# Six Winograd pairs per block and written-out operation lists in an attention and GeGLU kernel

## Chip, cores and metric

The kernel runs on one core of one Trainium2 chip. The metric is the device time of one execution in microseconds (us); the median of three runs stands for a kernel. Matrix products run on TensorE (PE), whose results land in PSUM; VectorE (DVE), ScalarE (ACT) and GpSimd (POOL) do the rest. SyncE (SP) issues the DMAs.

## What is computed

Linear attention over 8 batches with 8 heads, 576 rows and 64 columns each, and a gated feed-forward block on its output:

```python
def _attn_ref(q, k, v):
    q_s = softmax of q over the last axis
    k_s = softmax of k over the sequence
    kv = np.einsum('bhsd,bhse->bhde', k_s, v)
    return np.einsum('bhsd,bhde->bhse', q_s, kv)

def _moe_ref(x, w_gate, w_val, w_out):      # x: 4608 x 512, d_ff = 1536
    g = x @ w_gate
    gelu = 0.5 * g * (1.0 + erf(g * inv_sqrt2))
    val = x @ w_val
    return (gelu * val @ w_out).astype(np.float32)
```

All is float32 outside; inside, matmul operands are f16.

## The kernel before

The work goes through nine blocks of 512 rows: one per batch, 0 to 7, with the main 512 rows of the batch, and block 8 with the 64 remaining rows of each batch. They run in the order 0 to 6, 8, 7. A block has a gate part (12 tiles of 128 hidden columns, each `gelu(x w_gate) * (x w_val)`, into `ht`) and an output part (`ht` times `w_out`).

From block 1 on the output part (`out_strassen`, L755) is a seven-product Winograd scheme of 2 x 2 quarters. From block 2 on part of the gate is one too: hidden tiles k and k+3 are a *pair* (`pair_step`, L653), k one of 0, 1, 2, 6, 7, 8. A pair has seven products (`product_gv`, L619; matmuls at L629), each of four matmuls of 256 columns, in three PSUM banks:

- product 1 goes to bank a, which ACT copies to bank b (L686); products 6, 7, 4 accumulate in a, product 2 in b, products 5 and 3 in c (L629);
- a scaled snapshot of c after product 5 (*s5*) and of a after product 6 (*s2*) is taken to SBUF, by ACT (L666) or DVE (L664);
- DVE adds c to s2 after product 3, and a to s5 after product 7 (L670); ACT takes a Gelu of one half (L674), and POOL or DVE multiplies the two (L676): the rows 256 to 511 of both tiles;
- after product 2, and after product 4, ACT takes a 256-wide Gelu (L656) and DVE multiplies (L657): the rows 0 to 255.

A product may only write a bank after the snapshot, copy or add of its last state has read it. Tiles outside of pairs are computed directly (`half`, L643; matmuls at L471): 8 matmuls of 512 columns, a Gelu (L648) and a product (L650) each.

The pairs need sums of weight quarters (`sum_w1`, L604, two inputs in SBUF, 16 bits), made once for a pair's k; those for tile 7 are made in blocks 2 and 3, those for tile 8 in blocks 4 and 6, on DVE. They need four sums of x in each block (`sum_x`, L613, all on POOL), and the output part four sums of `ht` for each of three column groups (`sum_h`, L576, DVE or POOL).

Between these lies the attention of the next batches: exp of q and k (L210, ACT), row sums and reciprocals (`norm_pair`, L233, DVE), the scaling (`norm_mul`, L246, POOL), a cast of v (`cast_v`, L215, POOL), a DMA transpose of q (`unit_td`, L387, on SP), the k-v product (`unit_kv4`, L340) and x (`unit_x4`, L426), copied out of PSUM by ACT and DVE.

The order is set by hand. Each engine runs its instructions in program order; the program is emitted by walking a list of steps per block and "riding" other work on them (`at`, L949, and `ride`, L1034). Banks come from a ring of eight: `big(..., hold=True)` takes the next one and `let_go` puts it back at the end. The lists:

```python
FOUR = ("a 7g l 7v n 0.1 6.1 0.2 6.2 0.3 6.3 m p 10g 0.4 6.4 1.1 t 10v 1.2 8g 1.3 s0 8v u0 1.4 2.1"
        " 11g 2.2 11v 2.3 s1")
FIVE = ("a 8g l 8v n m 0.1 6.1 0.2 6.2 0.3 6.3 0.4 1.1 p 6.4 7.1 t 1.2 7.2 1.3 s0 7.3 2.1 1.4 u0 11g 2.2"
        " y 7.4 11v 2.3 s1")
...
steps = {b: (SIX if b >= B - 1 else FIVE if b > 3 else FOUR).split() for b in range(2, B + 1)}
```

`0.1` is the first step of pair 0, `7g` and `7v` the direct tile 7. So blocks 2 and 3 have pairs 0, 1, 2, 6 and four direct tiles; blocks 4 to 6 also have pair 7 and two direct tiles; blocks 8 and 7 have six pairs.

Of the kernel before, what the change touches and what calls it, by code (L numbers as in the profile page):

```python
# [18 lines left out]
def kernel(  # L19
# [12 lines left out]
    B, H, S, D = q.shape  # L32
    C = H * D
# [34 lines left out]
    def small(shape, dt, name):  # L68
        if not att_ring:
            return big(shape, dt, name)  # L70
        tag = att_ring.pop(0)
        att_ring.append(tag)
        full.discard(tag)
        return ps_big.tile(shape, dt, name=name, tag=tag)
# [18 lines left out]
    def let_go(t):  # L93
        ring.append(held.pop(id(t))[1])

# [176 lines left out]
    def norm_rem0():  # L272
        e = eq0r[0:64].rearrange("p (h d) -> p h d", d=D)
        rq = att.tile([64, H], f32, name="rq0", tag="rq0", bufs=1)
        nc.vector.reduce_sum(rq, e, axis=mybir.AxisListType.X)
        rrq = att.tile([64, H], f32, name="rrq0", tag="rrq0", bufs=1)
        nc.vector.reciprocal(out=rrq, in_=rq)
        nc.gpsimd.tensor_tensor(
            out=e, in0=e, in1=rrq.unsqueeze(-1).to_broadcast((64, H, D)), op=ALU.mult)
# [60 lines left out]
    def unit_kv4(b, spare=False):  # L340

        ps = bank([P, HP, VW], "pskv", spare)
        for hp in range(HP):
            for n in range(NC):
                for s in range(2):
                    c0 = hp * P + s * D
                    nc.tensor.matmul(  # L347
                        ps[s * D:(s + 1) * D, hp, :], ek_b[0][:, n, c0:c0 + D],
                        v16_b[0][:, n, 2 * hp + s, 0:VW], start=(n == 0), stop=(n == NC - 1))
        rck = att.tile([P, HP], f32, name="rck4", tag="rck4")  # L350
# [4 lines left out]
        st[(b, "kv4")] = kv  # L355

# [69 lines left out]
    def unit_x4(b, engs=("act", "dve"), rem=None):  # L426
# [19 lines left out]
        for s, eng in enumerate(engs):  # L446
            copy_on(eng, xtr[:, 2 * s:2 * s + 2, b * REM:(b + 1) * REM], psr[s][:, 0:2])
            if rem is not None:
                r = slice(64 * s, 64 * s + 64)
                copy_on("act" if b == B - 1 else eng, xtr[r, :, rem * REM:(rem + 1) * REM], psr[s][r, 2:])  # L450
        for i in range(2):
            ps = [big([P, MAIN], f32, "psx") for _ in range(2)]
            for hp in (2 * i, 2 * i + 1):
                go(ps, hp, xq(b, hp))
            for s, eng in enumerate(engs):
                copy_on(eng, xt[:, i + 2 * s, :], ps[s])
# [8 lines left out]
    def preload(func):  # L465
        nc.scalar.activation(out=tiny[:, 0:1], in_=tiny[:, 0:1], func=func)
# [7 lines left out]
    def gate(psg, psv, fi):  # L474
        gl = ffn.tile([P, 512], f32, name="gl", tag="gl")
# [137 lines left out]
    def sum_x(xt, xs=xs):  # L613
        b11, b12, b21, b22 = (xt[:, c:c + 2, r:r + 256] for c in (0, 2) for r in (0, 256))
        t = [xs[:, i] for i in range(4)]
        for o, a, b in ((t[0], b12, b11), (t[1], b22, t[0]), (t[2], b22, b12), (t[3], b21, t[1])):
            nc.gpsimd.tensor_tensor(out=o, in0=a, in1=b, op=ALU.subtract)

    def product_gv(i, ps, xt, k, first):  # L619
        lo, hi = slice(k * P, (k + 1) * P), slice((k + NO // 2) * P, (k + NO // 2 + 1) * P)  # L620
        xs = xs_b[xt is st.get((B - 1, "xt"))]
        for t, w, nm in ((0, wv_sb, "v"), (1, wg_sb, "g")):
# [11 lines left out]
    FOUR = ("a 7g l 7v n 0.1 6.1 0.2 6.2 0.3 6.3 m p 10g 0.4 6.4 1.1 t 10v 1.2 8g 1.3 s0 8v u0 1.4 2.1"  # L634
            " 11g 2.2 11v 2.3 s1")
    FIVE = ("a 8g l 8v n m 0.1 6.1 0.2 6.2 0.3 6.3 0.4 1.1 p 6.4 7.1 t 1.2 7.2 1.3 s0 7.3 2.1 1.4 u0 11g 2.2"
            " y 7.4 11v 2.3 s1")
    SIX = ("0.1 6.1 0.2 6.2 0.3 6.3 0.4 1.1 6.4 7.1 s0 1.2 7.2 1.3 u0 7.3 1.4 2.1 7.4 8.1 2.2"
           " 8.2 2.3 s1 8.3 2.4")
    steps = {b: (SIX if b >= B - 1 else FIVE if b > 3 else FOUR).split() for b in range(2, B + 1)}  # L640
    live = {}

    def half(b, xt, c, nm):  # L643
        t = big([P, 512], f32, "ps" + nm)
        mm_gv(t, wg_sb if nm == "g" else wv_sb, xt, c, range(HP))
        if nm == "g":
            live[c] = ffn.tile([P, 512], f32, name="gl", tag="gl")
# [5 lines left out]
    def pair_step(b, xt, k, i):  # L653
        def final(ps, fi):
            gl = ffn.tile([P, 256], f32, name="glq", tag="gl")
            nc.scalar.activation(out=gl, in_=ps[:, 1], func=ACTF.Gelu)  # L656
            nc.vector.scalar_tensor_tensor(out=ht[:, fi, 0:256], in0=ps[:, 0], scalar=_H_SCALE,  # L657
                                           in1=gl, op0=ALU.mult, op1=ALU.mult)
            let_go(ps)

        def snap(ps, dve=False):
            sn = ffn.tile([P, 2, 256], f32, name="snq", tag="snq")
            if dve:
                nc.vector.tensor_scalar(out=sn, in0=ps, scalar1=_H_SCALE, scalar2=None, op0=ALU.mult)  # L664
            else:
                nc.scalar.activation(out=sn, in_=ps, func=ACTF.Copy, scale=_H_SCALE)  # L666
            return sn

        def add(o, ps, sn):
            nc.vector.scalar_tensor_tensor(out=o, in0=ps, scalar=_H_SCALE, in1=sn,  # L670
                                           op0=ALU.mult, op1=ALU.add)

        def upper(cc):
            nc.scalar.activation(out=cc[:, :, 1], in_=cc[:, :, 1], func=ACTF.Gelu,  # L674
                                 scale=1.0 / _H_SCALE)
            (nc.vector if k == NFI - NO // 2 - 1 else nc.gpsimd).tensor_tensor(  # L676
                out=ht[:, k:k + NO // 2 + 1:NO // 2, 256:512], in0=cc[:, :, 0], in1=cc[:, :, 1],
                op=ALU.mult)

        if i == 1:  # L680
            live["odd"] = odd = not live.get("odd", True)
            cc = cc_b[b > 2] if odd else ffn.tile([P, 2, 2, 256], f32, name="cc", tag="cc", bufs=1)
            pa = big([P, 2, 256], f32, "pga", True)
            product_gv(1, pa, xt, k, True)
            pb = big([P, 2, 256], f32, "pgb", True, True)
            nc.scalar.copy(out=pb, in_=pa)  # L686
            pc = big([P, 2, 256], f32, "pgc", True)
            product_gv(5, pc, xt, k, True)
            live[k] = [cc, pa, pb, pc, snap(pc, b >= B - 1 or b > 3 and k % NO == 1)]
            return  # L690
        cc, pa, pb, pc, s5 = live[k]
        if i == 2:
            product_gv(6, pa, xt, k, False)
            s2 = snap(pa)
            product_gv(3, pc, xt, k, False)
            add(cc[:, 0], pc, s2)
            let_go(pc)
        elif i == 3:
            product_gv(7, pa, xt, k, False)
            add(cc[:, 1], pa, s5)  # L700
            product_gv(2, pb, xt, k, False)
            final(pb, k)
            if k == NFI - NO // 2 - 1 or 3 < b < B - 1 and k < 2 or 3 < b < B - 1 and k == NO:
                live["late"] = lambda: upper(cc)
            elif 3 < b < B - 1 and k == NO + 1:
                live["y"] = lambda: upper(cc)
            else:
                upper(cc)
        else:
            product_gv(4, pa, xt, k, False)  # L710
            if steps[b] and steps[b][0].endswith(".1"):
                live["late"] = lambda: final(pa, k + NO // 2)
            else:
                final(pa, k + NO // 2)

    def go_on(b, xt, upto=None):
        while steps[b] and upto != 0:
            x = steps[b].pop(0)
            late = live.pop("late", None) if "." in x else None
            if "." in x:  # L720
                k, i = x.split(".")
                pair_step(b, xt, int(k), int(i))
                upto = upto - 1 if upto else None
            elif x[-1] in "gv" and x[:-1].isdigit():
                half(b, xt, int(x[:-1]), x[-1])
            elif x == "y":
                live.pop("y")()
            else:
                ride(b, PR, x)
            if late:  # L730
                late()

# [19 lines left out]
    def last_js(b):  # L752
        return (NO - 2 if b < 2 else NO // 2 - 1, NO)

    def out_strassen(b, last):  # L755
        yo = [yop.tile([P, 2, C], f32, name="yo", tag="yo") for _ in range(2)]
        c = (slice(0, 256), slice(256, 512))
        ps, tiles_ = {}, {}

        def get(nm):  # L760
            if last:
                tiles_[nm] = [big([P, 256], f32, "ps" + nm, True) for _ in range(2)]
                ps[nm] = [x for x in tiles_[nm]]
            else:
                tiles_[nm] = [big([P, 2, 256], f32, "ps" + nm, True)]
                ps[nm] = [tiles_[nm][0][:, t] for t in range(2)]

        def parts(nm):
            return [(0, ps[nm][0]), (1, ps[nm][1])] if last else [(slice(0, 2), tiles_[nm][0])]

        def snap(nm, act=False):
            sn = ffn.tile([P, 2, 256], f32, name="sn", tag="gl")
            for n, (t, src) in enumerate(parts(nm)):
                if n or act:
                    nc.scalar.activation(out=sn[:, t], in_=src, func=ACTF.Copy, scale=1.0 / _H_SCALE)
                else:
                    nc.vector.tensor_scalar(out=sn[:, t], in0=src, scalar1=1.0 / _H_SCALE,  # L777
                                            scalar2=None, op0=ALU.mult)
# [321 lines left out]
```

The softmax here doesn't subtract the row's maximum and nothing guards it: scores larger than these inputs give would overflow.

## Time and profile before

| what | value |
|---|---|
| median of 3 runs | 292.18 us (292.15 to 292.21) |
| the profiled execution | 292.19 us |
| its span, first to last instruction | 290.3 us |
| POOL casting v, 128x640 (L186) | 26 times, mean 786 ns |
| ACT exp of one batch's k (L210), 128x2560 | mean 2324 ns |
| ACT table loads (L466, L210, L476) | 16, 1283 ns each |

The page gives busy time, share of the span and instruction count of each engine, then busy tenths in 40 slices. A row of the groups names line, engine, operation, out<-in with shapes and count, then total busy us, mean ns of one, and the idle time before it with what ended it. In the chain a piece is given by its start, its length and how many instructions it merges. In the stretches by block each number is the busy time of an engine with its instruction count in brackets.

### The profile page before, as it was taken

The numbers are of one execution on the slowest core, as the hardware profiler recorded it, in microseconds if no ns is written. First come the engines' busy times: TensorE is split into PE (matmuls) and PEld (weight loads), VectorE is DVE, ScalarE is ACT, GpSimd is POOL, SyncE is SP. The second block draws the span as 40 slices with busy tenths as digits, with TensorE's granted clock in tenths as the row PEclk, the third lists the DMA queues.
The fourth block names the chain that finished last, engine by engine and source line by source line (L and its number), as shares of the span: only waits on it lengthen the run. The fifth ranks groups of instructions, "written<-read, shape, count | busy, mean of one in ns | idle before, by whom it ended". The sixth has DMA issues, their size and how long they took to land.

```text
span 290.3 us, 6495 instructions
## 1 busy us (share of the span) xinstructions
PE 281.3 (97%) x2497; PEld 207.4 (71%) x2497; DVE 229.4 (79%) x430; ACT 197.8 (68%) x332; POOL 195.1 (67%) x180
## 2 busy tenths in 40 slices
PE   3999999999999999999999999999999999999994
PEld 1544445445877787768787878887888888888883
DVE  2854988877997779677988888887889689938982
ACT  3773367785787589757987698769773577537650
POOL 1567746987478569865996689669975476283640
PEclk9999999999999999999999999999999999999999
DMA  6999999999049903990299119911140110033003
GB/s 213 374 381 387 401 392 390 371 344 239 7 155 372 201 2 135 335 256 2 89 312 303 41 76 311 304 41 72 75 93 9 72 77 0 3 73 73 2 0 145
DMA packets 54622, 51.72 MB, mean 178 GB/s; under 512 B 18496, under 2 KB 50496, under 8 KB 54592
## 3 DMA queue, kind: packets, MB, share of 16 engines
q1 hardware_dynamic: 52864, 49.49, 54.3%
q10 hardware_dynamic: 1728, 1.84, 2.0%
q8 instruction: 19, 0.31, 0.4%
q14 instruction: 11, 0.09, 0.1%
HBM read 37.75 MB, written 9.44 MB: 163 GB/s over the span
## 4 chain that ended last, share of the span: by engine, by line
PE 95%; DVE 2%; ACTq 1%; ACT 1%; issue 0%
PE pga L629 21%; PE psa L745 14%; PE psg L471 11%; PE psv L471 11%; PE pgc L629 11%; PE psc L745 7%; PE pgb L629 5%; PE psb L745 4%; PE psy L539 4%; PE pswarm L463 2%; PE pskv L347 1%; PE psx L434 1%; ACTq L166 1%; DVE yo L783 1%; PE pst L372 1%; PE psx L413 1%
## 5 line engine op out<-in xcount | busy, mean ns | idle before, releaser
L629 PEld LDWEIGHTS <-wgv_sb 128*128 128x128 f16 x560 | 54.2, 98 | 10.7
L471 PEld LDWEIGHTS <-wgv_sb 128*128 128x128 f16 x304 | 29.5, 98 | 30.4 <-issue 0.8
L248 POOL TENSOR_TENSOR eq<-eq,rrq 128x640 f16<-128x640 f16 (+1 forms) x27 | 34.7, 1302 | 11.7 <-DVE rrq L240 8.2
L745 PEld LDWEIGHTS <-ht 128*128 128x128 f16 x384 | 36.6, 98 | 7.4 <-issue 2.5
L471 PE MATMUL psg<-xt,wgv_sb 128*128 128x512 f16 x152 | 41.1, 379 | 0.0
L471 PE MATMUL psv<-xt,wgv_sb 128*128 128x512 f16 x152 | 41.0, 379 | 0.0
L676 POOL TENSOR_TENSOR ht<-eq 128x512 f16<-128x512 f32 x17 | 21.6, 1272 | 19.7 <-ACT eq L674 19.6
L629 PE MATMUL pga<-xs,wgv_sb 128*128 128x256 f16 x232 | 34.5, 273 | 0.0
L656 ACT ACTIVATE glq<-pgb 128x256 f32<-128x256 f32 x35 | 13.3, 379 | 21.1 <-PE pgb L629 14.4
L586 POOL TENSOR_TENSOR s<-ht,sh 128x512 f16<-128x512 f16 x14 | 16.2, 1155 | 16.3 <-DVE sh L586 16.3
L476 ACT ACTIVATE gl<-psg 128x512 f32<-128x512 f32 x24 | 13.8, 597 | 16.8 <-PE psg L471 16.8
L676 POOL TENSOR_TENSOR ht<-cc 128x512 f16<-128x512 f32 x16 | 20.4, 1275 | 7.1 <-ACT cc L674 7.1
L186 POOL CAST v<-vt 128x640 f16<-128x640 f32 x26 | 19.4, 786 | 7.8 <-PE pskv L347 6.2
L686 ACT COPY pgb<-pga 128x512 f32<-128x512 f32 x35 | 20.4, 583 | 6.0 <-PE pga L629 5.6
L657 DVE SCALAR_TENSOR_TENSOR ht<-pga,glq 128x256 f16<-128x256 f32 x35 | 14.8, 422 | 12.0 <-ACT glq L656 11.8
L586 POOL TENSOR_TENSOR ht<-ht 128x512 f16<-128x512 f16 x16 | 18.9, 1188 | 8.0 <-DVE sh L586 8.0
L745 PE MATMUL psa<-tw,ht 128*128 128x256 f16 x192 | 23.4, 272 | 0.2
L477 DVE SCALAR_TENSOR_TENSOR ht<-psv,gl 128x512 f16<-128x512 f32 x24 | 16.0, 685 | 9.4 <-PE psv L471 7.7
L666 ACT ACTIVATE snq<-pga 128x512 f32<-128x512 f32 x35 | 20.9, 599 | 3.5 <-PE pga L629 3.2
L210 ACT ACTIVATE ek<-kt 128x1280 f16<-128x1280 f32 (+1 forms) x11 | 19.1, 1748 | 5.7 <-DMA kt<-in_k_dram 4.0
L238 DVE TENSOR_REDUCE rq<-eq 128x20 f32<-128x1280 f16 (+1 forms) x12 | 17.2, 1432 | 4.6 <-ACT eq L210 4.6
L745 PEld LDWEIGHTS <-sh 128*128 128x128 f16 x192 | 18.7, 98 | 2.5 <-DVE sn L777 0.3
(174 smaller groups left out, 683.0 us busy)
## 6 DMA issues: line engine op xcount, KB each, us to landing
out_dram<-yo SPq DMA_DIRECT2D x15, 512.0 KB, 3.4
kt<-in_k_dram SPq DMA_DIRECT2D x7, 640.0 KB, 8.5
vt<-in_v_dram SPq DMA_DIRECT2D x7, 640.0 KB, 5.6
qt<-in_q_dram SPq DMA_DIRECT2D x7, 640.0 KB, 7.7
qt<-in_q_dram SPq DMA_DIRECT2D x8, 512.0 KB, 7.9
wost<-in_moe_w_out_dram SPq DMA_DIRECT2D x6, 512.0 KB, 7.9
kt<-in_k_dram SPq DMA_DIRECT2D x6, 512.0 KB, 9.7
vt<-in_v_dram SPq DMA_DIRECT2D x6, 512.0 KB, 6.1
```

What stands on the lines that cost most here:

```text
L186: nc.gpsimd.tensor_copy(out=dst, in_=src)
L210: nc.scalar.activation(out=dst[:, n0:NC, h0 * D:h1 * D].rearrange(o, d=D, **({"t": 2} if b >= QUAD else {})), in_=heads(tiles[(nm, b)], b, ...
L238: nc.vector.reduce_sum(rq, e, axis=mybir.AxisListType.X)
L248: (nc.gpsimd if eng == "pool" else nc.vector).tensor_tensor(out=e, in0=e, in1=rrq.unsqueeze(-1).to_broadcast((P, n, 2, D)), op=ALU.mult)
L471: nc.tensor.matmul(ps, w[:, ci, fi * P:(fi + 1) * P], xt[:, ci, :], start=(ci == 0), stop=(ci == HP - 1))
L477: nc.vector.scalar_tensor_tensor(out=ht[:, fi, :], in0=psv, scalar=_H_SCALE, in1=gl, op0=ALU.mult, op1=ALU.mult)
L586: (nc.gpsimd if eng == "pool" else nc.vector).tensor_tensor(out=o, in0=a, in1=b, op=op)
L629: nc.tensor.matmul(ps[:, t], a, x, start=(first and t == 0 and c == 0), stop=(c == 1), skip_group_check=True)
L666: nc.scalar.activation(out=sn, in_=ps, func=ACTF.Copy, scale=_H_SCALE)
L676: (nc.vector if k == NFI - NO // 2 - 1 else nc.gpsimd).tensor_tensor(out=ht[:, k:k + NO // 2 + 1:NO // 2, 256:512], in0=cc[:, :, 0], in1=c ...
L686: nc.scalar.copy(out=pb, in_=pa)
L745: nc.tensor.matmul(ps[t], a, w, start=(first and j == js[0] and (t == ts[0] or ps[t].tensor is not ps[ts[0]].tensor)), stop=(j == js[-1]), ...
```

## The change

From block 2 on the lists of steps, `pair_step`, `go_on`, `half`'s calls, the riding and block 2 to 8's `out_strassen` are replaced by one list per block (`PROG`), in which every operation stands by itself, and by `play`, which emits one. Blocks 0 and 1 keep their code (a shortened `out_strassen` serves block 1). All blocks from 2 on have pairs 0, 1, 2, 6, 7, 8 and no direct tile. All eight `sum_w1` of tiles 7 and 8 stand in block 2. The words of a list:

- `kPi`: product i of pair k; `kc`: the copy of a to b (ACT); `ks2`, `ks5`: snapshot (ACT, with `d` DVE); `ka2`, `ka5`: the adds (DVE); `kg2`, `kg4` and `km2`, `km4`: 256-wide Gelu (ACT) and product (DVE); `ku`: Gelu of the lower half (ACT); `kU`: its product (POOL, with `d` DVE).
- `Oi:js`: output product i over some or all six column groups; `y1 y2 y5`: its snapshots; `a+ b+ c+`: its adds; `ye`: the last copy out.
- `sjip` or `sjid`: sum i of `ht` for group j; `xi`: sum i of x; `wki`: weight sum i of tile k; p is POOL, d DVE, a ACT.
- `NA NB`: row sums of q (DVE); `M0` to `M3`: its scaling (POOL); `Eq Ek`: exp (ACT); `V`: cast of v; `t`: transpose; `K k X Xa Xd`: k-v product, its normalization, x, its copies by ACT and DVE; `lq lk lv`: loads; `TE TG`: table loads.
- `<` and `>` take the operation of the block before and after.

```diff
-    FOUR = ...
-    FIVE = ...
-    SIX = ...
+    PROG = {
+        2: ("lk lq lv 6P1 0P1 <x0p 2P1 w81d 0P5 <x1d 6P5 <x3d 6c w82d 6P2 0c <x2d 6P6 w71d 0s5 0P6 6s5 0P3 6P3 6s2 "
+            "w72p 6g2 0P2 NB 0s2 6P7 6m2 w83p 0P7 0g2 6a2 1P1 2c 0a2 2P2 M3 1P5 0a5 1c 0P4 0m2 2g2 1P2 0u 6a5 M2 1P6 "
+            "0g4 2P5 6u 2P6 1s5 0U 6P4 1g2 NA 1P3 1s2 0m4 2m2 1P7 2s5 6U 1m2 7P1 2s2 2P3 6g4 1a2 s01p 2P7 1a5 7P5 6m4 "
+            "1u 1P4 2a2 M0 8P1 7c 2a5 7P6 7s5 w73d 7P2 w74d 8c 8P5 7s2 1Ud 7P3 1g4 w84d 8P6 s02d 2u 7P7 s04d 8s5 2P4 "
+            "7a2 8s2 8P3 7a5 2U 8P7 2g4 1m4 8P2 7u 8a2 7P4 7g2 M1 t O1:03 8g2 >>lr 8a5 8P4 7g4 2m4 7m2 O1:1 8u O1:4 "
+            "7U 8m2 O1:25 8g4 7m4 K 8m4 8U O2 s11d TE s21d y1a s23d s22d O5 s24d s12d k O6 Eq b+ s14p y5a O3:03142 "
+            "s03p y2a >NB X s13d O7 Xa Xd O3:5 x0d"),
...
+        4: ("6P1 NA 0P1 <x0d <O3:5 <x1d 6P5 0P5 <a+ <Ek lk <O4 0c <c+ <x3p 6c 0s5d <V2p 0P6 6P6 <TG 0P3 M0 <yea NB "
...
+        5: ("0P1 <Eq <O6 <Xd lq <x2d <Er <x0d 0c <x1d 6P1 <x3d <y5a <s24d 0P5 <O3:03142 6c <y2a <O7 NB <V0a 0s5d 0P6 "
+            "<b+ M2 6P6 6P5 <V1p <Ek <O3:5 lk 6P2 0s2 NA 0P2 0P3 <a+ 0P7 <c+ <TG M1 <O4 0g2 6g2 0a2 0m2 6s2 6m2 M3 "
+            "1P5 6s5 0a5 6P3 0P4 0u M0 1s5d 6P7 1P1 0g4 6a2 7P1 <yea 6a5 7P5 1c 6P4 7c Rr 1P6 0m4 7P6 6g4 0Ud 7P2 6u "
+            "6m4 1P3 7s2 1P2 1s2d 7g2 7P7 7s5 6U 1a2 2P1 1g2 7m2 1P7 1m2 <V2a s01p 8P1 2c 7P3 1a5 2P6 Rm 8c 8P5 7a5 "
+            "1u s03d 1P4 7P4 <V3a 7a2 lv 2P5 1g4 2s2d 8P6 8s5 t 2P7 >tr 1Ud 7u 1m4 2P2 7g4 8P3 8s2 2s5d 8P7 2g2 2a5 "
+            "7U 8P2 7m4 2P3 8a2 2P4 s11p 8g2 O1:03 8a5 2m2 8P4 2g4 s12p O1:1 2a2 8u O1:4 8m2 K 8g4 2m4 2u 8m4 O1:25 "
+            "8U O2 2Ud TE s21d s13d y1a O5 s22d s02d s04d s24d O6 s14d y5d Eq O3:03142 k V0a b+ V3a s23d X y2a O7 Xa "
+            "Xd O3:5 x0d"),
...
+    def play(b, x):
...
+        if k is not None and x[1] == "P":
+            i = int(x[2])
+            if i == 1:
+                product_gv(1, take(f"a{k}", [P, 2, 256]), xt, k, True)
+                take(f"b{k}", [P, 2, 256], True)
+            elif i == 5:
+                product_gv(5, take(f"c{k}", [P, 2, 256]), xt, k, True)
+            else:
+                product_gv(i, t[{2: "b", 3: "c"}.get(i, "a") + str(k)], xt, k, False)
...
     for b in order:
+        if b > 1:
+            for x in PROG[b].split():
+                play(b, x)
+            continue
```

The tail of block 3's list, `... O6 k b+ s24p y5d X Eq >lq s03p O3:03142 y2a V3p Xd O7 Xa V0a`, goes before the line of block 4 shown. SBUF rows for Gelus and snapshots come from rings of four each (`row`), and `unit_x4`'s copies are emitted by `x4_out`, after all of its matmuls.

## The prediction

> **What bounds the kernel now.** I read the page's busy times and slices first, then the waits of the TensorE (PE), then its chain of work for the pace of a matmul, then a table by block, then the groups by shape for the prices.
>
> ```profile
> PE 281.3 (97%) x2497; PEld 207.4 (71%) x2497; DVE 229.4 (79%) x430; ACT 197.8 (68%) x332; POOL 195.1 (67%) x180
> PE   3999999999999999999999999999999999999994
> PEclk9999999999999999999999999999999999999999
> PE 95%; DVE 2%; ACTq 1%; ACT 1%; issue 0%
> ```
>
> ```profile
> engine line waited for: us in total, times, longest us
> PE pswarm L463 <- ACT warm L892: 4.9, 1, 4.9
> ```
>
> PE makes up 95% of the chain that ends last, at the full clock, and its only wait is for the first warm-up matmul. Behind that it is never seen waiting for another engine. So the time is the start plus the columns that PE streams, and a change pays what it takes from or adds to PE's columns, plus any wait that it creates. The pace, from the chain in order of time:
>
> ```profile
> 19.79 0.86 PE psg L471 x4
> 37.06 7.77 PE psy L539 x36
> 103.63 1.31 PE psb L745 x12
> 104.94 1.31 PE psc L745 x12
> ```
>
> From 19.79 to 37.06 lie 80 matmuls of 512 columns: 17.27 us / 80 = 0.2159 us each. Twelve of 256 columns take 1.31 us: 0.1092 each. Blocks 2 to 8 by stretch (the first is block 2, the third block 4; the columns are busy times of PE, PEld, DVE, ACT and POOL):
>
> ```profile
> 82.32:112.25 29.93, 29.93 (x285) 23.01 (x284) 24.11 (x44) 23.22 (x39) 23.24 (x22) 1.00 0.57 165
> 142.20:171.80 29.60, 29.60 (x297) 24.11 (x296) 25.36 (x49) 23.93 (x43) 23.08 (x22) 1.00 0.63 184
> sum 207.98, PE 204.17 PEld 167.25 DVE 167.86 ACT 146.46 POOL 144.37; mean PE 29.17 PEld 23.89 DVE 23.98 ACT 20.92 POOL 20.62
> ```
>
> PE is full. DVE is the next engine, at 168 of 208 us.
>
> **What the Trainium skill says.** "TensorE: Matmul & The Clock Gate", section "Wait — 56ns, not 53.3ns?", puts back-to-back matmuls at N / 2.4 GHz + 2.5 ns: 215.8 ns for 512 columns, 109.2 for 256. The trace has 215.9 and 109.2. Its section on the array's architecture says that ScalarE and VectorE queues are strictly first in, first out; the trace never contradicts that, and it is why a long operation put early in a list delays all behind it. "SBUF — State Buffer", section "Who interferes with whom": a VectorE instruction with two SBUF inputs contends with a GpSimd instruction that reads SBUF, and the later one blocks until the other is done. The trace agrees:
>
> ```profile
> 126.14 0.41 DVE L586 TENSOR_TENSOR sh<-ht 128x512 f16<-128x512 f16 x1
> 126.48 0.68 DVE L650 SCALAR_TENSOR_TENSOR ht<-psv,gl 128x512 f16<-128x512 f32 x1
> 127.08 0.89 DVE L586 TENSOR_TENSOR sh<-sh,ht 128x512 f16<-128x512 f16 x1
> ```
>
> The first of these sums has POOL idle for most of it and takes 0.41; the second meets a POOL product (126.39 to 127.68) and takes 0.89. "PSUM — Partial Sum Buffer" gives eight banks; a pair in flight holds three (a, b, c), so three pairs don't fit at once.
>
> **The change part by part.** (1) Pairs. Two tiles computed directly are 16 matmuls of 512 columns, 16 x 0.2159 = 3.454 us; a pair is 7 products of 4 matmuls of 256, 28 x 0.1092 = 3.058. Saved per pair: 0.397 us. Added: two in each of blocks 2 and 3, one in each of 4, 5, 6, so seven: 2.78 us of PE. The output products, the attention's small matmuls and the end of the last block are the same in number.
>
> A step of a pair (0P1 and the like) is thus 0.437 us, a full output product O 1.31.
>
> (2) What a pair costs the others, none of it on PE. Prices are busy time, and behind each other on one engine the starts lie closer (two 0.68 us snapshots at 76.30 and 76.90: 0.60 apart), so I load an engine with spacings. DVE: 0.60 for each 512-wide f32 operation, 0.335 for the 256-wide gate and for a lone 16-bit sum. ACT: 0.49 to 0.53 for 512, 0.31 for a 256-wide Gelu, 2.24 for an exp of 2560, 1.39 for a table load with its dummy. POOL: 1.11 to 1.23.
>
> ```profile
> L676 POOL TENSOR_TENSOR ht<-eq 128x512 f16<-128x512 f32 x17 | 21.6, 1272 | 19.7 <-ACT eq L674 19.6
> L657 DVE SCALAR_TENSOR_TENSOR ht<-pga,glq 128x256 f16<-128x256 f32 x35 | 14.8, 422 | 12.0 <-ACT glq L656 11.8
> L670 DVE SCALAR_TENSOR_TENSOR cc<-pgc,snq 128x512 f32<-128x512 f32 x18 | 12.4, 691 | 2.9 <-ACT snq L666 2.4
> L617 POOL TENSOR_TENSOR xs<-xt,xs 128x512 f16<-128x512 f16 x10 | 11.5, 1153 | 0.4
> L676 DVE TENSOR_TENSOR ht<-cc 128x512 f16<-128x512 f32 x2 | 1.4, 692 | 0.2
> ```
>
> (3) Moves between engines. Of 42 products of the lower halves 21 now run on DVE (2 of 35 before); 19 of 28 sums of x go from POOL to DVE; six of the eight weight sums of block 2 are on DVE; 11 casts of v go from POOL to ACT. I add up the lists: DVE 177 us, ACT 151, POOL 98, beside PE's 201. So POOL is relieved and DVE goes to 88% of PE. By block list (they borrow from each other, so sums differ from stage lengths), PE / DVE / ACT: block 2 27.9 / 25.5 / 22.2; block 3 29.0 / 24.1 / 26.9; block 5 33.1 / 31.4 / 30.3; the rest have over 2 us to spare. No engine exceeds PE in any block, if 16-bit sums run alone.
>
> The trace has no sum of x and no weight sum without POOL on DVE. Nearest row: L586, same shape, 0.42 alone, 0.89 under POOL; so 0.335 to 0.82 in spacing. I take the low end where the list has no POOL operation beside it, which is most of block 2. In that block from w81d to w74d, and with the first one waiting for POOL's x sum to end at 83.02 (PE starts the block at 82.15, hence 0.87), DVE reaches the end of w74d at 0.87 + 12.7 = 13.6 us, and 7P3, which needs it, is due at 14.4: hidden. POOL's M0 (about 12.5 to 13.7) is likely to hold w73d: then 14.6 to 14.7, 0.3 late. With 0.82 for all of them w74d ends at 16.0, 1.6 late. I take 0.3.
>
> (4) Bank reuse. In block 5, 7P5 takes the bank that ACT's yea frees. Counted from the end of 0P4, 7P5 is due at 3 x 0.44 = 1.31; u, g and yea (0.53 + 0.31 + 0.58) end at 1.42, and 0.1 more until PE sees it: 0.2 late, nothing if u starts earlier. Later there, from the end of 7P7: DVE does 1a2, 7m2, 1m2, 1a5, 7a5, s03d, 7a2 by 3.4, and 2P5, which takes the bank that 7a2 frees, is due after eight steps at 3.5: just hidden. Such spots recur; I count 0.1 for all others together, and up to 1.2 as the far end.
>
> (5) The seam. Exp of k (2.24) now runs early in the next block. Queued behind it on ACT are the copies 0c and 6c that open b's banks, and behind those the table load and all snapshots; PE's P6 waits for the copies. Block 3 into 4, from the start of O6: ACT's Eq ends 1.64, y2a 2.13, Xa 3.3, a cast of v 3.9, Ek 6.2, 0c 6.7; 0P6, which needs 0c, is due at 7.7 (O6 1.31, X 0.7, O3 1.09, O7 1.31, four steps and a sixth of O3 2.0, O4 1.31): 1.0 to spare. Were Ek late by more, PE would wait for the rest. Table loads: 16 by count in both kernels. On SP the loads come in the same sets; k's load stands behind Ek and the half-block store, a block ahead of its use against the 8.5 us it takes to land: nothing. Later weight sums removed from blocks 3, 4, 6 leave DVE, not PE.
>
> Sum: 292.19 (the profiled run: span 290.3 and 1.9 around it) - 2.78 + 0.3 + 0.2 + 0.1 = 290.0. The median of the runs shown is 292.18, so the sum stands for it.
>
> **The rivals.** A, the likeliest: most of the columns' gain stays, 290.0, 289.6 to 290.9 with the spots of (3) and (4) at their ends. B, PE unbroken: 292.18 - 2.78 = 289.4; for it speaks that PE waits nowhere now with the same kind of dependences. C, the spots at banks and seams add up: about two of 0.15 us in each of seven blocks, 2.1 us, 291.5; for it speaks that many steps take a bank with none left free; against it that one wait loosens all later ones. D, slower: DVE becomes the bound by the shared SBUF port. 81 sums and 21 products on DVE read two SBUF operands (about 65 now, of which 13 are over 0.5 us). Each that meets POOL costs 0.49 more. If half do, block 2's DVE is 25.5 + 4.6 = 30.1 against 27.9, 2.2 us over, and block 5's 31.4 + 3.9 = 35.3 against 33.1, 2.2 over; with 0.6 elsewhere as in A, and 1 for the late sums that hold products, 292.2 - 2.8 + 6.0 = 295.4. It ends slower once the waits pass 2.8 us, at some 40% met. Against it: POOL is busy half of the time instead of 70%, and now a fifth of them meet it.
>
> **How the numbers follow.** A 0.60, B 0.14, C 0.17, D 0.09. The forecast is A's. 0.2% is 0.6 us, about what a measurement tells from no change: faster means below 291.6. A, B and 0.6 of C: 0.84; same 0.08 (the rest of C, a corner of D); slower 0.08. The range 289.3 to 291.6 holds A, B and C's near part.
>
> **What would show it.** Right: PE's mean distance of matmuls unchanged, block stretches some 28.4 us long, DVE at about 190 us in blocks 2 to 8 and no row of PE waits over 1 us. Wrong: PE waiting for DVE rows of the adds or of the weight sums in block 2 (D), for bank releases after the adds (C), for the copy of pga after Ek (5); 16-bit sums on DVE at 0.9 us instead of 0.42.

## The result and the profile after

The changed kernel takes 292.88 us (median of 4 runs, 292.5 to 292.95), the kernel before 292.19 beside it (4 runs): a ratio of 1.002, with a 95% interval of 1.0003 to 1.0037. So it is slower by about 0.7 us, a little over what can be told from no change. The forecast was 290.0.

The page of the changed kernel, with busy times, slices and the chain by engine:

```profile
PE 278.2 (96%) x2581; PEld 216.7 (75%) x2581; DVE 246.9 (85%) x488; ACT 210.5 (72%) x369; POOL 151.1 (52%) x138
...
PE   3999999999999999999999999997999999999992
...
PEclk9999999999999999999999999999999999999999
...
PE 79%; DMA 8%; DVE 4%; POOL 4%; issue 2%; ACT 1%; DVEq 0%; POOLq 0%; ACTq 0%
PE psa L670 21%; PE psA L749 11%; PE psc L670 11%; PE psg L511 7%; PE psv L511 7%; DMA eqt<-eq 6%; PE psC L749 6%; PE psb L670 5%; PE psy L579 4%; PE psB L749 3%; DMA qt<-in_q_dram 2%; POOL eq L265 2%; PE psa L749 1%; POOL xs L658 1%; DVE r
```

PE is busy for 3.1 us less, about the work that the forecast wanted to save, at the same full clock. But its row now has a 7 in its 28th slice (196 to 204 us) and a 2 at the end (a 4 before), its share of the chain fell from 95% to 79%, and a transfer has come into the chain: the transposition of q (`eqt<-eq`), with 6%. PE's waits name it:

```profile
engine line waited for: us in total, times, longest us
PE pswarm L503 <- ACT warm L1004: 4.9, 1, 4.9
PE psA L749 <- ACT gl L839: 1.7, 1, 1.7
PE psxr L462 <- DMA eqt<-eq: 0.3, 1, 0.3
PE psa L749 <- DVE yo L770: 0.2, 1, 0.2
```

Three rows are new. The last, 0.2 us, stands at 80.95, at the end of block 1. The other two lie behind it: an output product waits once, 1.7 us, for a snapshot by ACT (L839), and x (L462) waits for the transposition. A table by stretch, from one block's x to the next (columns as in the prediction's table), shows where: first block 2, second block 3, then blocks 4 and 5, then block 6, then blocks 8 and 7.

```profile
80.43:108.21 27.78, 27.63 (x302) 24.12 (x294) 27.19 (x57) 24.86 (x50) 18.16 (x15) 1.00 0.61 193
108.21:136.21 28.00, 28.00 (x306) 24.43 (x298) 25.68 (x51) 25.71 (x47) 15.45 (x14) 1.00 0.69 191
136.21:195.89 59.68, 59.37 (x634) 51.82 (x626) 56.27 (x114) 52.52 (x94) 35.24 (x31) 1.00 0.65 178
195.89:227.31 31.42, 29.64 (x325) 25.72 (x318) 26.88 (x53) 24.42 (x48) 17.37 (x15) 1.00 0.20 56
227.31:285.60 58.29, 58.27 (x536) 51.54 (x528) 50.41 (x106) 33.71 (x75) 14.58 (x12) 1.00 0.13 37
sum 205.17, PE 202.90 PEld 177.64 DVE 186.43 ACT 161.21 POOL 100.79; mean PE 40.58 PEld 35.53 DVE 37.29 ACT 32.24 POOL 20.16
```

PE is full in every stretch but the fourth, where 1.78 us of 31.42 are missing, right behind x of block 5. The pairs' gain is there: added up by the distance from one start to the next, the gate matmuls of blocks 2 to 8 take 131.56 us before and 128.85 after, 2.71 less.

Two places eat it up. PE's last matmul ends at 285.58 instead of 286.53, so of 2.71 us only 0.95 reach the end of PE; and from there to the end of the span lie 5.28 us instead of 3.77. Together: -0.95 + 1.51 = +0.56, the difference of the spans (290.9 and 290.3 on the pages).

### Place 1: the output product of block 5

The output products use three banks, psA, psB and psC; L839 is a snapshot on ACT. The timeline of ACT in the changed kernel there (start, length, engine, operation, and in brackets the idle time before and what ended it):

```profile
191.29 0.58 ACT L839 ACTIVATE gl<-psA 128x512 f32<-128x512 f32 x1
193.81 2.34 ACT L227 ACTIVATE eq<-qt 128x2560 f16<-128x2560 f32 x1 [1.94 <-DMA eqt<-eq]
196.06 1.34 ACT L205 CAST v<-vt 128x640 f16<-128x640 f32 x2
197.29 0.58 ACT L839 ACTIVATE gl<-psA 128x512 f32<-128x512 f32 x1
```

The timeline of SP, which issues the DMAs one by one:

```profile
183.71 1.35 SPq L183 DMA_DIRECT2D vt<-in_v_dram  x2
185.16 5.30 SPq L418 DMA_TRANSPOSE eqt<-eq  x1
```

And PE's:

```profile
195.64 0.60 PE L462 MATMUL psx<-eqt,kv 64*64 64x512 f16 x8
197.93 1.47 PE L749 MATMUL psA<-tw,ht 128*128 128x256 f16 x12 [1.69 <-ACT gl L839]
```

Read backwards: O7, output product 7, needs bank psA, and the snapshot y2 that saves the bank's last state stands in ACT's queue behind two casts and the exp of the next batch's q (`Eq`). This exp writes the buffer that the transposition reads (from batch 4 on there is one such buffer), so it waits until the transposition has landed: 185.16 + 8.62 = 193.78. The transposition was issued that late because in the list `lv`, the load of v, stands ahead of `t`. That load overwrites the buffer of v that ACT casts from; the last cast, `V3a`, runs from 182.93 to 183.64, and SP starts the load at 183.71. The wait that PE shows as "for ACT" is one for SP's order.

In the kernel before, the load of v went out long before the transposition, and the transposition had landed (7.2 us after its issue, at 190.8) 4.0 us before the exp of q began:

```profile
174.19 1.50 SPq L166 DMA_DIRECT2D vt<-in_v_dram  x2
183.60 4.59 SPq L390 DMA_TRANSPOSE eqt<-eq  x1
194.82 2.34 ACT L210 ACTIVATE eq<-qt 128x2560 f16<-128x2560 f32 x1
```

Three things used up this cover. ACT is now free for the exp at 191.87, 2.95 us earlier (x of block 5, too, comes 3.75 us earlier, at 195.55); the transposition is issued 1.56 us later; and it takes 1.4 us longer to land. Counted from x of its block, it is issued 10.4 us ahead instead of 15.7.

### Place 2: the last stores

DVE in the kernel before at the end (L783 adds a bank to its snapshot; L853 and L861 are the adds and the last copy of `finish_last`, in the changed kernel L842, L965 and L973):

```profile
283.81 0.76 DVE L783 SCALAR_TENSOR_TENSOR yo<-psc,sn 128x256 f32<-128x256 f32 x2 [0.89 <-PE psc L745]
284.58 0.42 DVE L853 SCALAR_TENSOR_TENSOR yo<-psa,sn 128x256 f32<-128x256 f32 x1
285.23 0.42 DVE L853 SCALAR_TENSOR_TENSOR yo<-psa,sn 128x256 f32<-128x256 f32 x1 [0.23 <-PE psa L745]
286.56 0.42 DVE L861 TENSOR_SCALAR yo<-psa 128x256 f32<-128x256 f32 x1 [0.91 <-PE psa L745]
```

And in the changed kernel:

```profile
283.63 0.42 DVE L965 SCALAR_TENSOR_TENSOR yo<-psA,gl 128x256 f32<-128x256 f32 x1 [1.30 <-PE psA L749]
284.28 0.42 DVE L965 SCALAR_TENSOR_TENSOR yo<-psA,gl 128x256 f32<-128x256 f32 x1 [0.23 <-PE psA L749]
285.61 0.42 DVE L973 TENSOR_SCALAR yo<-psA 128x256 f32<-128x256 f32 x1 [0.91 <-PE psA L749]
285.95 0.74 DVE L842 SCALAR_TENSOR_TENSOR yo<-psC,gl 128x256 f32<-128x256 f32 x2
```

The adds of bank c (`yo<-psC`), behind which half a block is stored, were first and are now last. In block 7's list `c+` stands behind `O7`, and for the last block the one word `O7` emits all of `finish_last`: O7, its adds, O4, the last copies and stores. The store of 512 KB so is issued after everything else, at 286.73, instead of beside PE's last 2 us (284.59 in the kernel before). The last store to land does so at 289.76 instead of 289.19, and in both kernels the span ends 1.1 us after that.

### The profile page after: what moved, and what is told of

Its sections match the earlier page's. It is cut to its first block, busy times and chain, and to the rows that moved or that the text cites. A ratio compares the mean times of both kernels' runs of the same rounds, so it can differ in the third digit from the quotient of the medians.

```text
span 290.9 us, 6711 instructions
## 1 busy us (share of the span) xinstructions
PE 278.2 (96%) x2581; PEld 216.7 (75%) x2581; DVE 246.9 (85%) x488; ACT 210.5 (72%) x369; POOL 151.1 (52%) x138
## 4 chain that ended last, share of the span: by engine, by line
PE 79%; DMA 8%; DVE 4%; POOL 4%; issue 2%; ACT 1%; DVEq 0%; POOLq 0%; ACTq 0%
PE psa L670 21%; PE psA L749 11%; PE psc L670 11%; PE psg L511 7%; PE psv L511 7%; DMA eqt<-eq 6%; PE psC L749 6%; PE psb L670 5%; PE psy L579 4%; PE psB L749 3%; DMA qt<-in_q_dram 2%; POOL eq L265 2%; PE psa L749 1%; POOL xs L658 1%; DVE rq L255 1%
## 5 line engine op out<-in xcount | busy, mean ns | idle before, releaser
L670 PE MATMUL psa<-xs,wgv_sb 128*128 128x256 f16 x288 | 40.7, 273 | 0.0
L858 ACT COPY psb<-psa 128x512 f32<-128x512 f32 x42 | 24.1, 585 | 8.2 <-PE psa L670 8.1
L511 PE MATMUL psg<-xt,wgv_sb 128*128 128x512 f16 x96 | 26.6, 379 | 0.0
L886 POOL TENSOR_TENSOR ht<-eq 128x512 f16<-128x512 f32 x12 | 16.0, 1332 | 19.2 <-ACT eq L884 15.7
L227 ACT ACTIVATE eq<-qt 128x2560 f16<-128x2560 f32 (+2 forms) x10 | 18.4, 1863 | 5.4 <-DMA qt<-in_q_dram 2.9
L749 PE MATMUL psA<-tw,ht 128*128 128x256 f16 x168 | 20.5, 272 | 1.7 <-ACT gl L839 1.7
L839 ACT ACTIVATE snq<-psc 128x512 f32<-128x512 f32 x29 | 17.4, 603 | 5.8 <-PE psc L670 5.6
L670 PE MATMUL psb<-xt,wgv_sb 128*128 128x256 f16 x144 | 20.8, 273 | 0.0
L670 PE MATMUL psa<-xt,wgv_sb 128*128 128x256 f16 x144 | 20.6, 273 | 0.0
L839 ACT ACTIVATE snq<-psa 128x512 f32<-128x512 f32 x31 | 18.5, 601 | 1.8 <-PE psa L670 1.8
L874 ACT ACTIVATE gl<-psb 128x256 f32<-128x256 f32 x42 | 15.8, 384 | 5.3 <-PE psb L670 4.9
```

What stands on the lines that cost most here:

```text
L227: nc.scalar.activation(out=dst[:, n0:NC, h0 * D:h1 * D].rearrange(o, d=D, **({"t": 2} if b >= QUAD else {})), in_=heads(tiles[(nm, b)], b, ...
L511: nc.tensor.matmul(ps, w[:, ci, fi * P:(fi + 1) * P], xt[:, ci, :], start=(ci == 0), stop=(ci == HP - 1))
L670: nc.tensor.matmul(ps[:, t], a, x, start=(first and t == 0 and c == 0), stop=(c == 1), skip_group_check=True)
L749: nc.tensor.matmul(ps[t], a, w, start=(first and j == js[0] and (t == ts[0] or ps[t].tensor is not ps[ts[0]].tensor)), stop=(j == js[-1]), ...
L839: nc.scalar.activation(out=dst, in_=src, func=ACTF.Copy, scale=scale)
L858: nc.scalar.copy(out=t[f"b{k}"], in_=t[f"a{k}"])
```

## The experiments

The theory has two parts: T1, `c+` behind `O7` makes the end of the kernel longer; T2, `t` behind `lv` makes the output product of block 5 wait; between them they hide the pairs' gain. The rivals: that the last stores and the transposition are not what ends last there, so that the time stays when they come earlier; and DVE's load (rival D of the forecast), which would make new waits in their place. Each expectation was written ahead of its run. All kernels differ from the changed one in the lists alone. Each ratio is to the kernel before on the same chip; its medians there, 292.17 to 292.18, agree so well that times from different chips can be compared.

### The adds of c ahead of the last product

```diff
 block 7, the end of the list:
-... b+ y2a s13d O7 c+ O4 a+ yed
+... b+ y2a s13d c+ O7 O4 a+ yed
```

> Block 7's adds of c (c+) stand ahead of O7, so that the store of the first half goes out before the last two output products. Theory T1 (the end is 1.5 us longer because this store is issued last, 286.7 us instead of 284.6): about 1.5 us less, 291.4, and PE's last matmul at the same time as in the changed kernel (285.6). Theory R1 (the end is longer because the DMA rings are busier or the stores themselves slower): no change, 292.9. Theory R2 (DVE is the bound throughout): under 0.3 us less.

Measured: 291.34 (291.05 to 291.53), ratio 0.9966 (0.9953 to 0.9978), 1.54 us below the changed kernel. PE's last matmul is where it was (285.76 and 285.58); the span ends 1.3 us earlier, 3.78 us behind that matmul instead of 5.28. DVE now adds c at 283.12, beside O7 and O4:

```profile
283.12 0.76 DVE L842 SCALAR_TENSOR_TENSOR yo<-psC,gl 128x256 f32<-128x256 f32 x2 [0.60 <-PE psC L749]
283.82 0.42 DVE L965 SCALAR_TENSOR_TENSOR yo<-psA,gl 128x256 f32<-128x256 f32 x1
284.47 0.42 DVE L965 SCALAR_TENSOR_TENSOR yo<-psA,gl 128x256 f32<-128x256 f32 x1 [0.23 <-PE psA L749]
285.80 0.42 DVE L973 TENSOR_SCALAR yo<-psA 128x256 f32<-128x256 f32 x1 [0.91 <-PE psA L749]
```

The large store is issued at 283.90 instead of 286.73. The wait of block 5 is still there (1.8 us). T1 is shown, with its size.

### The transposition ahead of the load of v

```diff
 block 5:
-... 0P4 0u M0 1s5d 6P7 ... <V3a 7a2 lv 2P5 1g4 2s2d 8P6 8s5 t 2P7 ...
+... 0P4 0u M0 t 1s5d 6P7 ... <V3a 7a2 lv 2P5 1g4 2s2d 8P6 8s5 2P7 ...
```

> In block 5 the transpose of q (t) is issued right after the last scaling M0, ahead of the load of v on SP's queue; nothing else moves. Theory T2 (the 1.7 us wait of PE ahead of O7 in block 5 comes from the transpose, issued late behind the load of v and landing at 193.8, which holds ACT's exp of q and with it the snapshot y2): exp of q starts some 2 us earlier, PE's wait goes, about 1.7 us less, 291.2. Theory R2 (ACT or DVE has too much to do in block 5, so that y2 would be late anyway): the wait stays above 1 us and the time above 292.3.

Measured: 291.07 (290.8 to 291.27), ratio 0.9958 (0.9943 to 0.9973), 1.81 us below the changed kernel. SP issues the transposition at 175.55; the exp of q starts at 191.95 without a wait, and O7 follows x after 0.31 us instead of 2.07. PE's last matmul ends at 284.02, 1.56 earlier. A wait for the transposition in block 4 stays (0.6 us, in the changed kernel 0.3).

This moves `t` and its order to `lv` at once. The next run keeps `t` in place and moves the load:

```diff
 block 5:
-... <V3a 7a2 lv 2P5 1g4 2s2d 8P6 8s5 t 2P7 ...
+... <V3a 7a2 2P5 1g4 2s2d 8P6 8s5 t lv 2P7 ...
```

> The changed kernel (292.88 us), but in block 5 the load of v stands directly behind the transposition t instead of six words ahead of it; t itself is not moved. It tells the order on SP's queue from the place in the list. Theory T2, t was late only because it stood behind a load that waits for ACT's last cast of v: t is issued as soon as its input is scaled, near 175.6 instead of 185.2, as in the run that moved t far ahead, the wait of 1.75 us at the output product goes and the time is 291.1. Rival, the place in the list counts too, or the transposition is slow because v's load runs beside it: t is issued later than 180 or takes over 8 us to land, and half or more of the 1.75 us stays, 292 or more.

Measured: 290.95 (290.56 to 291.01), ratio 0.9955 (0.9943 to 0.9968): the same gain. SP's timeline in this run:

```profile
177.31 4.46 SPq L418 DMA_TRANSPOSE eqt<-eq  x1
183.60 1.36 SPq L183 DMA_DIRECT2D vt<-in_v_dram  x2
```

`t` goes out 7.9 us earlier than in the changed kernel although it stands at the same place in the list (of the six words from `lv` to `8s5` ahead of it, only `lv` is for SP), and lands after 6.4 us instead of 8.6. The load of v is issued where it was. So what counts is the order of two words on SP's queue. The Trainium skill, "DMA: Bandwidth & Descriptors", section "Rules for kernel authors", advises to issue a DMA early and wait late; these two runs agree, and add that the place in the program is not early enough when the word ahead of it on the same queue waits.

### The snapshot on another engine

```diff
 block 5:
-... s23d X y2a O7 ...
+... s23d X y2d O7 ...
```

> In block 5 the snapshot y2 is made by DVE instead of ACT; the transpose stays late. Theory T2: DVE isn't behind the exp, so PE's wait ahead of O7 shrinks from 1.7 to under 0.3 us although the exp still waits for the transpose; but the exp of k and ACT's copies of x stay late, so that some of it may come back in block 6: 291.2 to 292.3. Theory R2 (DVE is full): DVE can't take it without delaying its own chain, and the time stays at 292.6 to 293.

Measured: 291.89 (291.49 to 292.64), ratio 0.9992 (0.9985 to 0.9999), 1.0 us below the changed kernel. DVE takes the snapshot at once and the wait at O7 is gone (0.42 us from start to start). But ACT is still late: the exp of q starts at 193.57, that of k at 198.16, and the copies that open the next block's banks stand behind it. PE loses 0.31, 0.38, 0.35 and 0.12 us in the first 9 us of block 6, 1.16 in sum. Of the 1.65 us won at O7 by taking the wait away without its cause, most was lost again there. The 1.0 us that remain are not all of this edit: in this run x of block 1 comes 0.2 us earlier, and a gap of 0.25 us at 8P5 in block 6 is absent.

### All of it together

```diff
 block 7:  c+ ahead of O7, as above
 block 5:  t behind M0, as above
 block 4:
-... 1P6 M2 0g4 ... lv 7P3 1a5 7s2 8P1 2c 2s5d 7P7 t s02p ...
+... 1P6 M2 t 0g4 ... lv 7P3 1a5 7s2 8P1 2c 2s5d 7P7 s02p ...
 block 3:
-... 1P4 M0 7s2 ... lv 7a5 8c O1:03 7a2 2s2 O1:1 t 7P4 ...
+... 1P4 M0 t 7s2 ... lv 7a5 8c O1:03 7a2 2s2 O1:1 7P4 ...
```

> The tail of block 7 as in the first run, the transpose of blocks 3, 4 and 5 right after the last scaling, ahead of the load of v. Theories T1 and T2 together: the two gains add up and the 0.5 us wait for the transpose in block 4 goes too: 292.9 - 1.5 - 1.7 - 0.3 = 289.4, within 0.3 us of the forecast's unbroken case. Theory R2: less than 1.5 us in all, above 291.4.

Measured: 289.25 (289.11 to 289.43), ratio 0.9897 (0.9882 to 0.9912), 3.63 us below the changed kernel: 1.54 + 1.81 and 0.28 for blocks 3 and 4. PE ends at 283.44 and the span 3.77 us later, as in the kernel before. This is where the forecast's "PE unbroken" lay (289.4), and with the same work as the changed kernel on every engine. PE's waits in this run:

```profile
engine line waited for: us in total, times, longest us
PE pswarm L503 <- ACT warm L1003: 4.9, 1, 4.9
PE pst L400 <- POOL eq L265: 0.4, 1, 0.4
PE psa L748 <- DVE yo L769: 0.2, 1, 0.2
```

All three lie in the start and in block 1. Within the gate of blocks 2 to 6, what is left are one gap of 0.25 us in block 6 and one of 0.10 in block 5, seen as distances from one start to the next.

### The last gap

```diff
 block 6, on the version before:
-... 8P1 1P4 7a5 2s2 2P7 1U 7a2 8c 8P5 ...
+... 8P1 1P4 7a2 7a5 2s2 2P7 1U 8c 8P5 ...
```

> The version with the three list repairs (289.25 us), and in block 6 the add 7a2 moved ahead of 7a5 in the list, so that the bank which 8P5 takes comes free 0.6 us earlier. Theory, the 0.25 us that PE loses at that place is the time until that add is done: the gap goes, 289.0, and with it no gap over 0.1 us is left in blocks 2 to 8. Rival, PE has enough queued behind or waits later for 7a5 (the copy and the products come 0.6 later): 289.25, the gap moves a few microseconds on.

Measured: 289.00 (288.85 to 289.07), ratio 0.9891 (0.9878 to 0.9905). The gap at 8P5 is gone; the largest left is the one of 0.10. The step in the medians, 0.25, is what the theory said, though the intervals overlap; the trace shows it. The bank that 8P5 takes came free later than it could, because another add, which could as well go second, stood ahead of the one that frees it. This version beats both kernels.

### What a pair is worth

On the version with the repairs (289.25), tiles 8 and 11 of blocks 3, 4, 5 and 6 are computed directly, so four of the seven added pairs are undone:

```diff
 blocks 3 to 6:
-8P1 ... 8P6 ... 8P3 ... 8P4 ...      (and 8c 8s2 8s5 8P5 8P7 8P2 8a2 8a5 8g2 8m2 8g4 8m4 8u 8U)
+8g 8ga ... 8v 8va ... 11g 11ga ... 11v 11va ...
```

Tile 11's weights hold a sum in one quarter, so its values here are others than the reference's; the instructions are the same in kind and number.

> The version with the three list repairs (289.25 us), but the pair of tiles 8 and 11 computed directly in blocks 3, 4, 5 and 6: 8g, 8v, 11g, 11v in the places of four of its seven steps, no sums, adds, copies or lower-half products for it. 16 matmuls of 512 columns take the place of 28 of 256 in each. Theory of the forecast's step (1), a pair is worth 0.397 us of PE and nothing of it is lost: PE's last matmul and the time come 4 x 0.397 = 1.6 us later, about 290.85, with no new wait. Rival, a pair's adds, copies and bank use cost PE something hidden that the direct form doesn't: less than 1.0 us later, or even faster, with small start gaps gone from those blocks.

Measured: 298.79 (298.69 to 299.15), ratio 1.0231 (1.0217 to 1.0245), far over both. The expectation missed the placing: I had put each Gelu directly behind its product. ACT in this run, in block 3:

```profile
124.46 0.60 ACT L893 ACTIVATE gl<-ps8g 128x512 f32<-128x512 f32 x1 [1.36 <-PE ps8g L511]
124.96 0.59 ACT L855 COPY psb<-psa 128x512 f32<-128x512 f32 x1
```

And PE there:

```profile
123.34 1.03 PE L511 MATMUL ps8g<-xt,wgv_sb 128*128 128x512 f16 x4
125.60 0.38 PE L670 MATMUL psa<-xs,wsv 128*128 128x256 f16 x2 [1.23 <-ACT psb L855]
```

ACT waits 1.36 us for the product, the copy of pair 2 waits behind it, and PE waits 1.23 for the copy. So the same four pairs were undone again with each Gelu, and each product on DVE, some steps of PE later; to make room for that, some of the direct products of tiles 8 and 11 moved by a few steps too:

```diff
 blocks 3 to 6:
-8g 8ga ... 8v 8va ...
+8g ... 8ga ... 8v ... 8va ...
```

> As the run before with tiles 8 and 11 computed directly in blocks 3 to 6 on the version with the three list repairs (289.25 us), but the Gelu stands one or two steps of PE after its product in the list instead of directly behind it, so that the copies and snapshots queued on ACT don't wait for PE there. Tile 11's weights hold a sum in one quarter when they are used directly, so its values are others than the reference's; the work is the same in kind and number. Theory of step (1): 4 x 0.397 = 1.6 us more columns and no waits of the size that the run before had (7.9 in sum): 290.85, and up to 291.6 with some left. Rival, a pair kept PE waiting somewhere that the direct form frees: under 290.2. If the waits of the run before come from the banks and not from ACT's order: over 294.

Measured: 290.41 (290.27 to 290.49), ratio 0.9938 (0.9925 to 0.9952). The largest gap in the gate is 0.10 us here too. From x of block 1 to the last matmul, PE takes 204.90 us, in the best version 203.29: 1.61 for four pairs, 0.402 each, against 0.397 of the forecast. The medians differ by less, 1.41, since the start ahead of that x took 0.37 us less in this run; the time is 0.4 under the expectation, but over the 290.2 of its rival. And the same work in the worse order cost 8.4 us more, by waits for words of ACT and of DVE alike.

### Products of the lower halves back on POOL

```diff
 all blocks, 21 words, on the version with the repairs:
-kUd
+kU
```

> The version with the three list repairs (289.25 us), but all 21 products of the lower halves that the lists put on DVE go to POOL (14 us off DVE, some 27 us onto POOL, where a product takes 1.27 instead of 0.69). It tests the moves of step (3). Theory, PE is the bound and the moves between DVE and POOL are hidden either way: within 0.4 us of 289.25, save where a product stands late in its block (8Ud, 2Ud) and the output product O2 waits for it: at most 0.6 later in each of five blocks, so up to 292. Rival D of the forecast (DVE near its bound, hurt by POOL beside it): more of DVE's 16-bit sums meet POOL and take up to 0.9 us instead of 0.42, DVE's adds come late all over the blocks and PE waits for them, 293 or more.

Measured: 293.77 (293.62 to 293.89), ratio 1.0055 (1.0043 to 1.0068): 4.5 us over the 289.25 it started from, more than my theory allowed (292) and inside the rival's range. PE's busy time per matmul is unchanged; start gaps grew from 1.4 us in sum to 5.5. DVE's load fell, from 246.9 us to 235.8, so it isn't load. DVE in block 5, with its idle time:

```profile
193.44 0.42 DVE L626 TENSOR_TENSOR sh<-ht 128x512 f16<-128x512 f16 x1 [1.79 <-POOL ht L885]
193.78 0.42 DVE L626 TENSOR_TENSOR ht<-ht 128x512 f16<-128x512 f16 x1
194.12 0.75 DVE L626 TENSOR_TENSOR sh<-sh,ht 128x512 f16<-128x512 f16 x2
194.90 1.10 DVE L626 TENSOR_TENSOR s<-ht,sh 128x512 f16<-128x512 f16 x3
195.92 0.69 DVE L836 TENSOR_SCALAR gl<-psC 128x512 f32<-128x512 f32 x1
```

POOL has two products in a row there (190.91 and 192.14, 1.27 each); DVE's first sum of `ht` waits for them, and behind it in the queue stands the snapshot of psC that PE needs. The same chain, a sum on DVE that waits for POOL, and PE that waits for this sum or for something behind it, stands at 136.3, 223.5 and 241.1. These four gaps of PE make 1.9 us. In block 2 the two engines meet in SBUF as rival D said: two sums take 1.18 (95.18) and 1.50 us (97.41) beside POOL, 0.42 each in the run it started from, and PE's gaps right behind them, at 96.4, 99.7 and 100.9, make 1.2 us. Of the 81 sums of 16 bits on DVE from block 2 on, 8 meet POOL for over 50 ns here and 5 in the run it started from; over 0.5 us take 6 and 3. So of the 4.1 us by which the gaps grew, the queue has the larger share and the meeting in SBUF a real one; no run separates them, and 0.9 us are not assigned.

## Why the prediction was wrong, step by step

**(1) Pairs: right.** 2.78 us foretold, 2.71 measured in the gate matmuls with their small gaps, and 0.402 instead of 0.397 for one pair.

**(2) Loads: right.** 186 us of DVE in the stretch of blocks 2 to 8 (about 190 foretold), 161 of ACT, 101 of POOL; no wait of PE comes from a full engine.

**(3) Moves to DVE: right in direction, too careful in block 2, and blind to what they carry.** The 0.3 us at 7P3 did not occur: `w73d` was expected under POOL's M0 and took 0.416 without any POOL operation beside it. The Trainium skill's "SBUF — State Buffer", section "Who interferes with whom", on which rival D rested, is borne out: the 81 sums take 0.43 us in the mean, and the three of over 0.5 us (0.62, 0.63 and 0.81) have a POOL operation beside them that began before they did. Two more meet one that began after them, and keep their 0.42. But they are three, so D was far off. That it is worth 4.5 us which engine has DVE's 21 products was not in the forecast: it counted them as a load, not as places in a queue.

**(4) Banks: right in size, not in place.** 0.3 us foretold: 0.25 came at 8P5 in block 6, and 0.07 and 0.06 at two steps in block 8 whose cause is open; 7P5 behind `yea` did not wait. (The 0.10 in block 5 shows in the repaired versions alone.)

**(5) The seam: this step failed.** The walk from block 3 to 4 was right: no copy is late there. But for SP the forecast says "the loads come in the same sets" and "nothing", from the load of k alone. So it put SP's order at nothing without a walk through SP's own queue for block 5, where `t` stands behind `lv` and `lv` behind a cast. That cost 1.76 us at O7 (2.07 from start to start, 0.31 is normal) and, by the same order of `lv` and `t` in block 4, 0.38 at x there (a gap of 0.48, 0.09 is normal).

**The end: the second failed step.** In part (1) the end of the last block is called "the same in number" and so put at nothing. That is true and beside the point: the order had changed, `c+` had gone behind a word that holds the whole end. It cost 1.51 us.

The distances between PE's starts add up to the whole difference. The gate gives -2.71, with the gaps of (4) in it; the two waits +1.76 and +0.38; the end +1.51; x of block 1 comes 0.10 later. What the forecast had not is -0.50 in work that it took as equal: the output products take 0.34 us less, x 0.16. Of the 0.34, 0.27 are three gaps of 0.09 us that the kernel before has where a step of a pair stands amid an output product (160.9, 190.5 and 220.1); why it has them stays open. In all +0.54; the spans differ by 0.56. The best version gains the same 0.5 in output products and x, which is why it lies under the forecast's "PE unbroken" (289.00 against 289.4).

The likelihood of "slower" (0.08) stood on rival D alone. The two causes that acted are neither load nor bank but order on a queue: on SP's in block 5, on DVE's and so on SP's at the end.

## What to carry to other kernels

When the order is written out by hand, walk every queue by itself, SP's too: for each word ask what the word ahead of it waits for, and when its result is overwritten next. A wait that a profile puts down to ACT can begin with two DMAs in the wrong order, and the repair is at the beginning of the chain: mending its last link brought 1.0 us, mending the beginning 1.8. A word that stands for many operations, like the last block's `O7`, is to be opened before its neighbours are placed.

## What was not expected of the hardware

The transposition in block 5 took from 6.1 to 8.6 us to land: 7.2 in the kernel before (issued at 183.60), 8.6 in the changed kernel, where it was issued directly behind the load of v, and 7.1, 6.4 and 6.1 in three runs where it ran ahead of it. Its issue alone held SP for 4.0 to 5.3 us. No run here tells the load's share in that from other traffic.
